# Keys loaded one head at a time, and turned by a product with the unit matrix instead of a two-head transpose

## Chip, cores, metric

One NeuronCore of a Trainium2 chip runs the whole program. The metric is the device time of one execution in microseconds, as a median of several runs. TensorE is called PE here (its weight loads PEld), VectorE DVE, ScalarE ACT, GpSimd POOL and SyncE SP; SP issues nearly all transfers.

## What is computed

Attention with four batches, twelve heads, 448 positions and a head size of 64. The heads are mixed before and after the softmax, and the result runs through a two-layer network with SiLU.

```python
scores = scale * np.matmul(q, k.transpose(0, 1, 3, 2))     # q, k, v: (4, 12, 448, 64) float32
scores = np.einsum('bhij,hg->bgij', scores, w_pre)          # mix of heads
scores = scores - np.max(scores, axis=-1, keepdims=True)
attn = np.exp(scores)
attn = attn / (np.sum(attn, axis=-1, keepdims=True) + 1e-09)
attn = np.einsum('bhij,hg->bgij', attn, w_post)             # second mix
x = np.matmul(attn, v)                                      # then (batch*seq, heads*size)
h = x @ w_in
out = (h * (1.0 / (1.0 + np.exp(-h)))) @ w_out
```

## The kernel before

The program has three parts. An **opening** (to about 28 us) brings queries and keys of batch 0 into the core and makes the first scores. The **mixing part** (to about 420 us) walks through four batches of four query tiles each (120 or 100 query rows), in groups of ten query rows. The **network** (from there to the end) is a chain of 128x448 products, L624.

In the mixing part every pair of groups takes these steps: L399 mixes the scores of all heads (`mix_pair`, into `pp`), L405 takes the row maxima on DVE, L409 the exponentials on ACT, L437 mixes them again (`mix_pair_again`, into the one tile `pa`), and L446 copies `pa` out on ACT. Between them stand pieces of other work: L368 multiplies finished weights with values (`values`), L339 makes the scores of the next tile (`scores`, into `pqk`), L344 and L346 copy these to a buffer `st` (six of them), and a transfer, L351, spreads `st` over the partitions of a tile `g`, from which L399 reads. A buffer `st` is free again once its transfer has landed.

What the change touches is the way keys come in. `load_k_pair` (L238 to L249) issues one transfer for each head of a pair. Position 4p+j of a head goes to partition p (112 partitions, j from 0 to 3), so a head is 1 KB in a row in memory for each partition. In the core the two heads of a pair lie interleaved: for each j first 64 numbers of one head, then 64 of the other. The tile is `kn`, or a part of one of the four value tiles `v` while that is not in use, so the trace names some of these transfers and products by `v`. `prep_k` (L264 to L278) then makes four transposes a pair with PE: for each j a block of 112 partitions by 128 columns (both heads) becomes 128 partitions by 112 columns of a bank `pt`. L274 and L277 split that into a rounded part `kh` and a rest `kl`.

There are 24 pairs of heads. The six of batch 0 are loaded and turned in the opening, between the first scores. The six of each later batch are loaded (lists `early`) and turned (lists `work`) while the batch before is being mixed, at places that `put` fixes by group number; the order of the instructions on each engine is written out by the loop over the groups. SP works through its transfers in program order, and each of them waits on the semaphore of the eighth transfer before it, so that about eight are on the way at a time.

Of the kernel before, what the change touches and what calls it, by code (L numbers as in the profile page):

```python
# [8 lines left out]
F32 = mybir.dt.float32  # L9
# [13 lines left out]
def raw(ap):  # L23

    return ap.bitcast(F32)
# [78 lines left out]
def talking_heads_then_silu_mlp(  # L104
# [11 lines left out]
    nc = tc.nc  # L116
    ctx.enter_context(tc.manual_schedule())
    B, H, S, D = q.shape
# [8 lines left out]
    JT = 112  # L127
    NJ = S // JT
# [20 lines left out]
    ident = const.tile([128, 128], F32, name="ident")  # L149
# [18 lines left out]
    def pool(name, bufs, stack=ctx, **kw):  # L168
        return stack.enter_context(tc.tile_pool(name=name, bufs=bufs, **kw))
# [13 lines left out]
    nat = pool("nat", 2, early_p)  # L183
# [12 lines left out]
    def bank(p, name):  # L196
        if p is ps_a:
            turns.append(name)
            return pa[:, len(turns) % 2]
        return p.tile([128, 512], F32, name=name, tag="bank")  # L200

    v_tiles = [v2_p.tile([KV, 4, NJ, D], F32, name="v4", tag="v4") for _ in range(4)]
# [35 lines left out]
    def load_k_pair(b, h, queues=(nc.sync, nc.sync)):  # L238
        if h >= 4 if b == 0 else h // 4 != 1:
            x = (b * H + 8) // 4 % 4 if b else h // 4 - 1  # L240
            if x in zeroed:
                zeroed.remove(x)
            t = v_tiles[x][:JT, h % 4:h % 4 + 2].rearrange("p i j d -> p (i j d)")
            t = t.rearrange("p (j i d) -> p j i d", i=2, j=NJ)
        else:
            t = nat.tile([JT, NJ, 2, D], F32, name="kn", tag="kn")
        kns[b, h] = t
        for i in range(2):
            queues[i].dma_start(out=t[:, :, i, :], in_=k[b, h + i].rearrange("(p j) d -> p j d", p=JT))  # L249

    def load_v_quad(b, h):
        x = (b * H + h + 8) // 4 % 4
# [11 lines left out]
    def prep_k(b, h):  # L264

        pt = bank(banks[0], "pt")
        kn = kns.pop((b, h))
        for j in range(NJ):
            nc.tensor.transpose(pt[:, j * JT:(j + 1) * JT], kn[:, j].rearrange("p h d -> p (h d)"), ident[:JT, :JT])  # L269

        kh, kl = ks[b, h] = [k2_p.tile([128, S], F32R, name=x, tag=x) for x in ("kh", "kl")]

        def take_high():
            nc.scalar.copy(out=kh, in_=pt[:, :S])  # L274

        def take_low():
            nc.vector.tensor_sub(out=kl, in0=pt[:, :S], in1=raw(kh))  # L277
        return [(take_high, take_low)]  # L278
# [196 lines left out]
    for n in range(1, len(seq)):  # L475
        p0, p1 = first[n - 1], first[n]
        spread = (0, 0, 0, 0, 2, 2) if n == 1 else (-6, -5, -4, -2, -1, 0) if p1 - p0 == 12 else (-6, -5, -4, -3, -2, -1)
        for h in range(0 if n > 1 else 2 * NE, H, 2):
            i = p0 + spread[h // 2]
# [7 lines left out]
    for n, (b, ti) in enumerate(seq):  # L487
        if n:
            p0 = first[n - 1]
            if n > 2:  # L490
                put(first[n - 2], lambda n=n: load_q(n)[0](), lead=7, w=2.1)
            for hg, i in ((0, p0 - 9), (1, p0 - 8)):
                if n > 1:
                    put(i, prep_q, n, hg)
            if ti == 0:
                c0 = first[n - 2]
                for h, i, lead in zip(range(0, H, 2), (0, 1, 3, 5, 7, 9), (10, 10, 11, 12, 5, 6)):
                    put(c0 + i, load_k_pair, b, h, lead=lead, w=1.2)
                    put(c0 + i, prep_k, b, h)
        if ti == 0:  # L500
            for h in range(0, H, 4):
                put(first[n] + ((5, 6, 8) if n else (15, 16, 18))[h // 4], load_v_quad, b, h, lead=2, w=1.8)
# [23 lines left out]
    for h in range(0, 6, 2):  # L526
        load_k_pair(0, h, (nc.sync, nc.scalar))
    loads[1]()
    for h in range(6, H, 2):
        load_k_pair(0, h)  # L530
    steps = [(prep_q, 0, 0), (prep_k, 0, 0), (prep_k, 0, 2)]
    for h in range(0, H, 2):
        if h + 4 < H:
            steps.append((prep_k, 0, h + 4))
        steps += [(scores, 0, h)]
        if h == 0:
            steps.append((prep_q, 0, 1))
# [313 lines left out]
    for s, (kind, m, u, a) in enumerate(steps):  # L851
# [14 lines left out]
        p = None  # L866
        if s >= len(phs):
            p = bank(ps_h, "ph")
# [58 lines left out]
```

## Time and profile before

| | |
|---|---|
| median of 3 runs | 872.0 us (870.98 to 878.78) |
| the profiled execution | 876.44 us, span 874.7 us |
| PE busy | 828.4 us, 95% of the span |
| PEld, DVE, ACT, POOL busy | 656.0, 625.4, 526.5, 406.4 us |
| transfers | 132.89 MB in 162343 packets; 50409 packets under 512 B |

The span is the time between the first and the last instruction of the profiled execution. Busy shares are means over three parts with different limits, so they have to be read by stretches; the granted clock of PE stands beside them. A busy PE is one with a product in its pipeline, and how many products it gets through is read from their starts.

### The profile page before, as it was taken

Reading aid. Unit: us, or ns where it says so; the run is one execution under the profiler, and the core shown is the slowest. Engines: PE = TensorE matmul, PEld = TensorE weight load, DVE = VectorE, ACT = ScalarE, POOL = GpSimd, SP = SyncE. Lnnn points to the kernel's source line nnn. Section 1 sums busy time; section 2 is a strip of 40 time slices with the busy share of each in tenths; the row PEclk is TensorE's granted clock in tenths of the full one; section 3 lists DMA queues with packets and bytes.
Section 4 is the critical chain, followed back from the end, with each engine's and each line's share of the span. In section 5 each row is a group of like instructions: output and inputs, shape, how many; then the busy total and the mean of one; then the engine's idle time right before and its main releaser. Section 6 shows DMA issues by size and latency. Waiting matters only on the chain.

```text
span 874.7 us, 27490 instructions
## 1 busy us (share of the span) xinstructions
PE 828.4 (95%) x11058; PEld 656.0 (75%) x11058; DVE 625.4 (71%) x1218; ACT 526.5 (60%) x1178; POOL 406.4 (46%) x681
## 2 busy tenths in 40 slices
PE   7797999899998999899899999999999999999997
PEld 5355666567666666666599999988899889999986
DVE  5453777468775777675878899999988689984332
ACT  4575778578786878677756653324694245343242
POOL 6231445355454645463877577557742233133020
PEclk7999899899999999999999999999999999999999
DMA  7569677887788787874635453355331142112234
GB/s 143 167 182 193 185 212 218 219 216 196 209 242 229 220 219 211 228 214 151 188 104 184 144 167 118 118 151 155 107 94 49 35 114 71 38 49 73 73 85 106
DMA packets 162343, 132.89 MB, mean 152 GB/s; under 512 B 50409, under 2 KB 155861, under 8 KB 162215
## 3 DMA queue, kind: packets, MB, share of 16 engines
q1 hardware_dynamic: 158809, 129.39, 53.0%
q8 instruction: 87, 1.43, 0.7%
q0 software_dynamic: 544, 1.03, 0.5%
q10 hardware_dynamic: 2862, 0.71, 0.4%
q14 instruction: 41, 0.34, 0.1%
HBM read 64.01 MB, written 27.53 MB: 105 GB/s over the span
## 4 chain that ended last, share of the span: by engine, by line
PE 75%; DVE 9%; DMA 7%; ACT 4%; issue 2%; SPq 2%; POOL 1%; ACTq 0%; POOLq 0%; DVEq 0%
PE ph L624 41%; PE pa L437 8%; PE pp L399 8%; PE po L368 7%; PE pqk L339 7%; DMA g<-st 4%; ACT e L409 2%; DVE nm L405 1%; DVE g L824 1%; PE pt L269 1%; PE ptt L844 1%; ACT at L446 1%; DVE op L630 1%; DMA v<-in_v 1%; DVE cg L92 1%
## 5 line engine op out<-in xcount | busy, mean ns | idle before, releaser
L624 PE MATMUL ph<-op,wh 128*128 128x448 f32 x924 | 221.5, 368 | 2.4 <-DVE g L834 1.8
L610 POOL TENSOR_TENSOR wl<-wl,wh 128x512 fp32r<-128x512 f32 x84 | 122.0, 1467 | 152.8 <-ACT wh L609 152.3
L624 PEld LDWEIGHTS ph<-op,wh 128*128 128x128 f32 x924 | 171.6, 188 | 18.1 <-DVE g L834 2.1
L405 DVE TENSOR_REDUCE nm<-pp 128x1 f32<-128x448 f32 x184 | 106.1, 618 | 76.1 <-PE pp L399 75.7
L425 POOL TENSOR_SCALAR wr<-wpost,r 128x60 f32<-128x60 f32 x184 | 70.7, 397 | 177.5 <-DVE r L422 139.0
L409 ACT ACTIVATE e<-pp,nm 128x448 f32<-128x448 f32 x184 | 115.4, 631 | 51.1 <-DVE nm L405 48.8
L437 PEld LDWEIGHTS pa<-wr,e 64*64 64x64 f32 (+1 forms) x5888 | 96.7, 131 | 44.9 <-issue 26.5
L437 PE MATMUL pa<-wr,e 64*64 64x60 f32 (+1 forms) x5888 | 108.6, 219 | 14.4 <-ACT at L446 8.6
L624 PE MATMUL ph<-op,wl 128*128 128x448 f32 x462 | 118.9, 366 | 0.0
L399 PE MATMUL pp<-g,wpre 64*64 64x448 f32 x736 | 104.9, 591 | 9.6 <-ACT e L409 5.7
L66 POOL TENSOR_TENSOR cg<-cw,cg 128x256 f32<-128x256 f32 x96 | 75.8, 790 | 76.6 <-DVE cw L63 73.5
L624 PEld LDWEIGHTS ph<-op,wl 128*128 128x128 f32 x462 | 86.7, 188 | 7.5 <-POOL wl L610 0.5
L446 ACT COPY at<-pa 120x960 f32<-120x960 f32 x92 | 89.9, 978 | 3.2 <-PE pa L437 3.2
L368 PE MATMUL po<-at,v 120*64 120x120 f32 (+1 forms) x1536 | 88.1, 268 | 1.8 <-DMA v<-in_v 1.5
L368 PEld LDWEIGHTS po<-at,v 120*64 120x64 f32 x1536 | 77.4, 139 | 14.6 <-issue 5.1
L609 ACT CAST wh<-wl 128x512 fp32r<-128x512 f32 x84 | 51.1, 617 | 54.3 <-DMA wl<-wo_dram 27.2
L344 DVE COPY st<-pqk 120x448 f32<-120x448 f32 (+1 forms) x89 | 55.0, 618 | 36.5 <-PE pqk L339 17.5
L90 ACT ACTIVATE cg<-cg,ebias 128x256 int32<-128x256 int32 x96 | 49.6, 516 | 44.2 <-DVE cg L86 43.0
L92 DVE SCALAR_TENSOR_TENSOR cg<-cw,cg 128x256 int32<-128x256 int32 x96 | 56.2, 586 | 16.4 <-ACT cg L90 16.0
L624 PE MATMUL ph<-x,wh 128*128 128x448 f32 x252 | 64.7, 365 | 0.0
L339 PEld LDWEIGHTS pqk<-kh,qh 64*120 64x120 f32 (+1 forms) x186 | 19.0, 179 | 50.0 <-issue 17.7
L339 PE MATMUL pqk<-kh,qh 64*120 64x448 f32 (+1 forms) x186 | 47.6, 467 | 6.8 <-ACT st L346 5.4
(122 smaller groups left out, 1379.0 us busy)
## 6 DMA issues: line engine op xcount, KB each, us to landing
g<-st SPq DMA_DIRECT2D x132, 210.0 KB
cw<-in_moe_w_in SPq DMA_DIRECT2D x48, 256.0 KB
cw<-in_moe_w_out SPq DMA_DIRECT2D x48, 256.0 KB
wi_dram<-cg SPq DMA_DIRECT2D x24, 448.0 KB
wo_dram<-cg SPq DMA_DIRECT2D x24, 448.0 KB
wl<-wi_dram SPq DMA_DIRECT2D x42, 256.0 KB
wl<-wo_dram SPq DMA_DIRECT2D x42, 256.0 KB
g<-st SPq DMA_DIRECT2D x48, 175.0 KB
```

The lines of the kernel that those rows point to most:

```text
L66: nc.gpsimd.tensor_mul(out=e, in0=m, in1=e)
L92: nc.vector.scalar_tensor_tensor(out=e, in0=hi, scalar=-2 ** 31, in1=e, op0=ALU.bitwise_and, op1=ALU.bitwise_or)
L339: nc.tensor.matmul(ps[i][:m, :S], lhsT=q_[rows, hh, :m], rhs=k_[rows], start=(step == 0), stop=(step == 2))
L368: nc.tensor.matmul(po[i * D:(i + 1) * D, c * m:(c + 1) * m], lhsT=vs[b, h][:, i, j, :], rhs=ats[n][:, j, h + i, :m], start=(j == 0), stop= ...
L399: nc.tensor.matmul((self, other)[r].p[HP * c:HP * (c + 1), :S], lhsT=wpre[rows], rhs=gs[self.n][rows, o // R + c * np + p, :], start=True, ...
L405: nc.vector.tensor_reduce(out=self.nm, in_=self.p[:GP, :S], axis=AX.X, op=ALU.max, negate=True)
L409: nc.scalar.activation(out=self.e, in_=self.p[:GP, :S], func=AF.Exp, bias=self.nm, scale=1.0, accum_out=sums)
L425: nc.gpsimd.tensor_scalar(out=g.wr, in0=wpost.rearrange("p g i -> p (g i)"), scalar1=r[:, i:i + 1], scalar2=1.0, op0=ALU.mult, op1=ALU.mult)
L437: nc.tensor.matmul(half[64 * c:64 * c + m, s, j * GH:(j + 1) * GH], lhsT=g.e[rows, j * JT + c * JH:j * JT + c * JH + m], rhs=g.wr[rows], s ...
L446: nc.scalar.copy(out=ats[self.n].rearrange("p j g t -> p (j g) t")[:, :, o:o + 2 * R].rearrange("p x (c i) -> p x c i", i=RH), in_=pa[:KV] ...
L610: nc.gpsimd.tensor_sub(out=wl, in0=raw(wl), in1=raw(wh))
L624: nc.tensor.matmul(p[:, :T], lhsT=w, rhs=x, start=(n == 0), stop=(n == len(todo) - 1))
```

## The change

Each transfer now puts the four rows of a head that belong to a partition next to each other, so the two heads of a pair lie behind one another and a partition gets 1 KB of a head in one piece. The block of both heads for one j is then no longer one piece of 128 columns. Instead of one transpose for each j there are two ordinary float32 products, one for each head: the stationary operand is the head's block (112 partitions, 64 columns), the moving one the unit matrix of 112 columns, and the result goes to the head's half of the 128 partitions of `pt`.

```diff
-            t = v_tiles[x][:JT, h % 4:h % 4 + 2].rearrange("p i j d -> p (i j d)")
-            t = t.rearrange("p (j i d) -> p j i d", i=2, j=NJ)
+            t = v_tiles[x][:JT, h % 4:h % 4 + 2]
         else:
-            t = nat.tile([JT, NJ, 2, D], F32, name="kn", tag="kn")
+            t = nat.tile([JT, 2, NJ, D], F32, name="kn", tag="kn")
         kns[b, h] = t
         for i in range(2):
-            queues[i].dma_start(out=t[:, :, i, :], in_=k[b, h + i].rearrange("(p j) d -> p j d", p=JT))
+            queues[i].dma_start(out=t[:, i], in_=k[b, h + i].rearrange("(p j) d -> p j d", p=JT))
...
         for j in range(NJ):
-            nc.tensor.transpose(pt[:, j * JT:(j + 1) * JT], kn[:, j].rearrange("p h d -> p (h d)"), ident[:JT, :JT])
+            for i in range(2):
+                nc.tensor.matmul(pt[i * D:(i + 1) * D, j * JT:(j + 1) * JT], lhsT=kn[:, i, j], rhs=ident[:JT, :JT], start=True, stop=True)
```

On PE the opening reads so (a row is a run of equal instructions, with the size of the result; `v_131` is a value tile that holds keys):

```order
-L269 MATMUL pt<-ident,kn 128x112 x8
-L269 MATMUL pa<-ident,v_131 128x112 x4
+L269 MATMUL pt<-ident,kn 64x112 x16
+L269 MATMUL pa<-ident,v_131 64x112 x8
 L339 MATMUL pqk<-kh,qh 120x448 x2
 L339 MATMUL pqk<-kh,ql 120x448 x2
 L339 MATMUL pqk<-kl,qh 120x448 x2
```

Nothing changes place there; every set of four transposes has become eight products at the same point. On SP the first transfers were these (the size is partitions by pieces):

```order
L297 DMA qn<-in_q 120x6x64
L249 DMA kn<-in_k 112x4x64 x2
L249 DMA v_131<-in_k 112x4x64
L297 DMA qn<-in_q 120x6x64
L249 DMA v_131<-in_k 112x4x64 x2
L249 DMA v_132<-in_k 112x4x64 x4
```

In the changed kernel the same six rows read:

```order
L297 DMA qn<-in_q 120x6x64
L248 DMA kn<-in_k 112x256 x2
L248 DMA v_131<-in_k 112x256
L297 DMA qn<-in_q 120x6x64
L248 DMA v_131<-in_k 112x256 x2
L248 DMA v_132<-in_k 112x256 x4
```

The number and the order of the transfers are the same; each one has 112 pieces of 256 numbers where it had 448 of 64. DVE, ACT and POOL keep their instructions and their order.

## Rows read from the trace of the kernel before

**Rows 1.** The page: busy time of PE; shares of the last-ending chain by line.
```profile
PE 828.4 (95%) x11058; PEld 656.0 (75%) x11058; DVE 625.4 (71%) x1218; ACT 526.5 (60%) x1178; POOL 406.4 (46%) x681
...
PE ph L624 41%; PE pa L437 8%; PE pp L399 8%; PE po L368 7%; PE pqk L339 7%; DMA g<-st 4%; ACT e L409 2%; DVE nm L405 1%; DVE g L824 1%; PE pt L269 1%; PE ptt L844 1%; ACT at L446 1%; DVE op L630 1%; DMA v<-in_v 1%; DVE cg L92 1%
```

**Rows 2.** Busy times by stretch; last three columns PEclk, DMA share, GB/s.
```profile
4.00:8.00 4.00, 2.11 (x15) 1.52 (x15) 1.67 (x4) 1.99 (x5) 3.58 (x8) 0.98 1.31 186
8.00:12.00 4.00, 3.98 (x19) 2.83 (x19) 1.63 (x4) 1.72 (x5) 0.33 (x1) 0.50 1.01 148
12.00:16.00 4.00, 4.00 (x18) 2.50 (x19) 2.66 (x6) 1.85 (x4) 1.12 (x2) 0.50 0.52 145
...
75.00:88.00 13.00, 8.46 (x211) 6.16 (x207) 3.57 (x10) 5.77 (x16) 1.69 (x6) 0.94 0.98 213
88.00:100.00 12.00, 12.00 (x210) 7.43 (x210) 8.00 (x19) 8.39 (x22) 4.32 (x9) 0.79 0.66 186
...
300.00:320.00 20.00, 19.54 (x426) 13.92 (x427) 15.44 (x37) 16.61 (x40) 11.20 (x26) 1.00 0.87 230
```

**Rows 3.** Timeline of PE from 299 us: start, length, engine, line, tiles, shape, count.
```profile
299.84 0.60 PE L269 MATMUL pt<-ident,v 112*128 112x112 f32 x4
300.37 0.98 PE L399 MATMUL pp<-g,wpre 64*64 64x448 f32 x8
301.28 1.86 PE L368 MATMUL po<-at,v 120*64 120x120 f32 x32
303.07 1.16 PE L437 MATMUL pa<-wr,e 64*64 64x60 f32 x64
...
304.52 0.55 PE L269 MATMUL pt<-ident,kn 112*128 112x112 f32 x4
305.00 0.98 PE L399 MATMUL pp<-g,wpre 64*64 64x448 f32 x8
...
306.91 1.16 PE L437 MATMUL pa<-wr,e 64*64 64x60 f32 x64 [0.46 <-ACT at L446]
```

**Rows 4.** Timeline of PE from 255 us.
```profile
255.36 1.59 PE L368 MATMUL po<-at,v 120*64 120x100 f32 x32
```

**Rows 5.** The chain of work that ended last, opening: start, length, what.
```profile
2.73 5.16 DMA v<-in_k
...
8.03 0.98 PE pa L269 x4
...
18.04 1.33 PE pqk L339 x11
...
23.56 4.88 DMA g<-first
```

**Rows 6.** PE busy from 8 to 12 us with L269 alone, then PEclk.
```profile
8.00:12.00 4.00, 1.93 (x8) 0.50 1.01 148
```

**Rows 7.** Transfers from 0 to 8 us: ACT's queue, packets, MB, share.
```profile
q10 hardware_dynamic: 1392, 0.34, 22.9%
```

**Rows 8.** Transfers from 410 to 414 us: SP's queue.
```profile
q1 hardware_dynamic: 245, 0.24, 18.5%
```

**Rows 9.** Issues of the first scores' transfers by SP: shortest/median/longest ns, first and last start.
```profile
L351 SPq DMA_DIRECT2D g<-first x18: 748/748/1442, 11.0 to 28.8; - x18
```

**Rows 10.** Issues of key transfers by SP, the same columns.
```profile
L249 SPq DMA_DIRECT2D v<-in_k x31: 562/630/2118, 2.7 to 306.7; - x31
```

**Rows 11.** Timeline of SP to 110 us: issues, with their length.
```profile
65.16 5.12 SPq L249 DMA_DIRECT2D v<-in_k  x4
...
75.95 3.09 SPq L249 DMA_DIRECT2D kn<-in_k  x2
...
80.94 5.19 SPq L351 DMA_DIRECT2D g<-st  x6
```

**Rows 12.** Timeline at 87 us: who waited for what before it started.
```profile
87.31 0.53 ACT L346 COPY st<-pqk 100x448 f32<-100x448 f32 x1 [1.12 <-DMA g<-st]
...
87.89 0.69 PE L339 MATMUL pqk<-kh,qh 64*100 64x448 f32 x1 [4.54 <-ACT st L346]
```

## The prediction

> **What bounds the kernel now.** I read the page first: PE is busy for 95% of the span and holds the first places of the chain, and the transposes of the keys, L269, are 1% of that chain, some 9 us [rows 1]. So the change works on a small sum, and what it can cost or give back is a few microseconds on either side of it. Then I read the windows by stage, because the transposes lie in four places only: six sets of four in the opening and six in each of three stretches of the mixing part. In those stretches PE is the bound: from 300 to 320 us it is busy for 19.54 of 20 us [rows 2], and its timeline shows one piece of work behind the other [rows 3]. There a microsecond more on PE is a microsecond more in the end, and a transfer that lands sooner gives nothing.
>
> Two other places are not bound by PE. In the opening, PE waits for the third pair of heads: the chain holds 5.16 us of a key transfer and then PE from 8.03 us to the last scores, which SP then spreads, the last of them landing 4.88 us after 23.56 us [rows 5]. From 75 to 88 us the transfers are at a share of 0.98 and PE is busy for 8.46 of 13 us [rows 2]; the scores at 87.89 us waited 4.54 us, for a buffer that its transfer had not yet emptied [rows 12]. The reader is to see that key transfers stand in SP's queue just ahead of those that empty the buffers: four in 5.12 us, then two in 3.09 us, and only at 80.94 us the first of the six [rows 11].
>
> **What the change costs on PE.** A set of four transposes takes from its start to that of the next work 0.53 us after L437 and 0.48 us after the query transposes (299.84 to 300.37, 304.52 to 305.00) [rows 3]; I take 0.51. The new set is eight float32 products. The trace has their like in L368: blocks of 120 partitions by 64 columns, in turn on the one and the other half of the columns, with 120 or 100 columns moving. Such a float32 product has two rows in the trace, so 32 rows are 16 products. With 120 columns they take 1.79 us to the next start (301.28 to 303.07; the row's 1.86 us has a tail of 0.07 that overlaps) [rows 3], with 100 columns 1.59 - 0.07 = 1.52 us [rows 4], that is 0.0135 us a column. At 112 columns 32 rows come to 1.68 us, and a new set of 16 rows to half of that, 0.84 us, if all of it scales with their number. The line through the two points leaves 0.17 us at no columns; if that is a fixed cost of the change from one kind of work to another, a set is 0.76 + 0.17 = 0.93 us. I take 0.88, the middle. The extra is 0.88 - 0.51 = 0.37 us a set; the bounds are 0.84 - 0.53 = 0.31 and 0.93 - 0.48 = 0.45.
>
> There are 18 such sets in the mixing part. Three of them, one per batch, stand shortly before a place where PE waits for ACT for some 0.46 us (306.91, behind the set at 304.52) [rows 3]; that wait covers their extra, so long as ACT, which has two splits and a copy of `pa` to do there, stays the last to come. Fifteen sets at 0.37 us are 5.6 us; one of them lies between 88 and 100 us, where the granted clock is 0.79 in the mean [rows 2], so I say 5.7 us. Bounds: 15 x 0.31 = 4.7 and 18 x 0.45 = 8.1.
>
> DVE and ACT read `pt` as before and get it 0.37 us later; what they feed (`kh`, `kl`) is used groups later, so that costs nothing as long as ACT has its slack. The only new waits are on PE, one for each head instead of one for both; the head that lands last decides as before.
>
> **What the transfers give back.** On ACT's queue, which carries almost only keys in the first 8 us, 1392 packets fill 22.9% of 16 engines for 8 us, so one of 256 B takes 21 ns [rows 7]. From 410 to 414 us 245 packets of 1 KB fill 18.5% of 4 us, 48 ns each [rows 8]. So 1 KB of keys goes from 84 ns to 48 ns of one engine: a head of 448 rows from 448 x 21 / 16 = 0.59 us of all engines to 112 x 48 / 16 = 0.34 us.
>
> In the batches at 174 and 285 us nothing waits for these transfers, so there it is 0 us.
>
> From 60 to 88 us the queue is full. Eight heads save 8 x 0.25 = 2.0 us of transfer time, and SP stands 5.12 + 3.09 us in six of their issues [rows 11], where six at the median of 0.63 us would be 3.8 us [rows 10], so some 4.4 us of it is stall. The six transfers that empty the buffers then start 2 to 4 us sooner, and the wait of 4.54 us [rows 12] shrinks by as much. I take 2.5 us, the lower end plus a little of the clock: PE idled before its clock fell, and it is at 0.79 from 88 to 100 us [rows 2], which is 12 x 0.21 = 2.5 us of work lost. With a shorter idle stretch some of that need not happen. Bounds: nothing (if other transfers fill the room at once) and 4.0 + 2.5 = 6.5 us. What is late next is the value loads in the same queue.
>
> In the opening three pairs, 6 x 112 KB, must land before 8.03 us; they save 6 x 0.25 = 1.5 us, and I take 1.4. From there the price depends on the clock. From 8 to 16 us PE is busy for 7.98 of 8 us, and its clock is 0.50, the lower level of 1.2 GHz [rows 2]; in the first half of that 1.93 us are L269 [rows 6]. At that level the four sets behind the wait take about 1 us each now (0.98 for the first) [rows 5] and would take 1.7 (twice 0.84), so 0.7 us more each: 2.8 us more, less 1.4, is 1.4 us; the last pairs' scatters, though, are paced by SP rather than by PE, so about half of it, 0.7 us, reaches the end. At the upper level the work between 8.03 and 18.04 us, 10.0 us now [rows 5] and 12.8 with the extra, would take 6.4. Then SP is the next in line: the first scores come some 2 us sooner (1.4 by the keys, the rest by the clock), the first scatter is issued at 9.0 instead of 11.0 us, and eleven more at 0.75 us [rows 9] with a little between them put the twelfth at 18 to 19 us instead of 23.56 [rows 5], a gain of about 5.
>
> Here a rule of the Trainium skill bears on the choice. TensorE: Matmul & The Clock Gate, Part 4, says that work in transpose mode does not count as PE being busy in the way products do, so that the full clock does not engage for it. The rows at 8 to 16 us agree: a PE that is busy for 3.98 of 4 us stays at 0.50 while half of that is transposes [rows 2, 6]. By the rule the products would raise the clock, and the opening would gain about 5 us; without it, it would lose about 0.7.
>
> From the rows alone: the clock fell behind 4 to 8 us, where PE was busy 2.11 of 4 us [rows 2], and with keys 1.4 us sooner and sets twice as long PE would have nearly no gap there. So I take a gain, but not all of it: 3.5 us. Bounds: a loss of 0.7 and a gain of 5.
>
> **The sum.** 5.7 - 2.5 - 3.5 = -0.3 us against the profiled execution's 876.44 us, so 876.1 us. That execution lies 4.4 us above the median of the three runs; applied to the median of 872.0 the forecast is 871.7, rounded to 872. A run of this kernel differs from the next by up to 7.8 us, so about 1% is what a measurement can tell from no change.
>
> **The rivals.**
>
> First, that the two halves of the columns do not run beside each other. Then eight products take twice 0.88 us, 1.25 us a set more than now, since 16 rows follow one another: 18 x 1.25 = 22.5 us in the mixing part, where no wait covers that much, and some 4 us in the opening, less 2.5 us from 60 to 88 us: about 896 us. It makes the kernel slower by over 1% from a set of 1.3 us on: (8.7 + 6.0 given back) / 18 is 0.8 us more than 0.51. Against it stands L368, which has the same shape and does overlap; for it, that L368 adds up over j in one place while here every product starts anew in another. The Trainium skill has a rule on this side: TensorE: Matmul & The Clock Gate, Terms, calls transpose mode four times faster for float32. Four times the 0.48 us of a set would be 1.9 us, and the mixing part about 18 x 1.4 = 25 us longer. No row here sets a transpose beside a product of the same block.
>
> Second, that the products keep the clock up in the opening and that the room in the queue from 60 to 88 us is worth its full price. This is what the rule of Part 4 would do here, together with the upper bound of the queue: 4.7 - 6.5 - 5 = -6.8, so 865 us.
>
> Third, that the transfers are hidden anyway: other packets fill the room from 60 to 88 us and the clock in the opening falls as before. Then 5.7 to 8.1 plus 0.7 is left: 878 to 881 us.
>
> **How the numbers follow.** The forecast has 0.52, the third rival 0.20, the second 0.18, the first 0.10. The range reaches to the second and the third, with their bounds and some 2 us for the medians themselves: 863 to 881 us; the first rival and the far ends are left out. Faster by over 1% (below 863.3) would need the second rival with luck on top: 0.10. Slower by over 1% (above 880.7) is the first rival and the worst of the third: 0.14. Within 1%: 0.76.
>
> **What the profile after would show.** Right, if a set of L269 takes 0.84 to 0.96 us to the next start in the stretch around 300 us; if the key issues on SP take less than half as long between 65 and 79 us and the wait before the scores at about 87 us is 2 us or so; if the first pairs are turned without a wait and the clock from 8 to 16 us is above 0.50. Wrong on PE, if a set takes 1.7 us; wrong on the transfers, if the first mix of the opening still starts at 28 us and the wait at 87 us is still above 4 us. The sum would be wrong if the sets' extra hid behind ACT in more than three places, or if the mixing part changed its waits at the tile boundaries, which no row here prices.

## The result and the profile after

The changed kernel takes 882.0 us (median of 22 runs, 872.6 to 886.5), the kernel before 877.5 us in 22 runs beside it (871.0 to 887.8). The ratio is 1.0054 with a 95% interval of 1.0031 to 1.0077: 4.7 us more, 2.7 to 6.8. Ratios here, unlike the medians, leave out the runs that lie over 1.5% above the fastest of the same kernel (five of 22 before, two of 22 after; the means of all runs differ by 2.9 us). The forecast was 872 us with a range to 881 and 0.3 us of gain.

Two things lie in the miss. The kernel before stood at 872.0 us by the three runs that the forecast was applied to, and at 877.5 by 22: 5.5 us of the 10 are the sampling of its median. The rest is the change, 4.7 us by the ratio. The change itself is within 1%, as forecast, but its sign is clear of the interval, and it is the third rival's.

The page of the changed kernel (its profiled execution took 882.34 us), the lines that answer to [rows 1]:

```profile
span 880.6 us, 28064 instructions
PE 833.7 (95%) x11346; PEld 663.7 (75%) x11346; DVE 625.7 (71%) x1218; ACT 527.9 (60%) x1178; POOL 407.1 (46%) x681
...
PE ph L624 39%; PE pa L437 9%; PE po L368 8%; PE pp L399 7%; PE pqk L339 7%; DMA g<-st 4%; PE pt L269 2%; ACT e L409 1%; DVE op L630 1%; DVE g L824 1%; DVE nm L405 1%; DMA qn<-in_q 1%; DVE cg L92 1%; PE ptt L844 1%; ACT at L446 1%
```

PE has 288 rows of products more, 24 sets by 12, and L269 went from 1% to 2% of the chain. The windows by stage, to be laid beside [rows 2]:

```profile
4.00:8.00 4.00, 3.90 (x49) 3.25 (x50) 1.35 (x3) 1.39 (x4) 3.58 (x8) 1.00 1.16 222
8.00:12.00 4.00, 4.00 (x55) 2.88 (x53) 3.11 (x6) 2.96 (x7) 1.18 (x2) 1.00 0.46 120
12.00:16.00 4.00, 4.00 (x50) 2.99 (x45) 3.04 (x10) 2.62 (x6) 0.27 (x1) 1.00 0.65 183
75.00:88.00 13.00, 11.48 (x279) 7.90 (x269) 5.74 (x16) 6.66 (x16) 1.89 (x5) 1.00 0.82 224
88.00:100.00 12.00, 11.79 (x260) 8.33 (x256) 8.99 (x21) 10.21 (x26) 6.07 (x15) 1.00 0.78 206
```

Both places that were not bound by PE look better, just as the forecast wanted: from 8 to 16 us the clock is 1.00 instead of 0.50, and from 75 to 88 us PE is busy for 11.48 of 13 us instead of 8.46. Still the kernel is slower. The timeline of PE around 304 us, where [rows 3] had 0.48 us for a set after the query transposes:

```profile
304.06 0.99 PE L269 MATMUL pt<-ident,kn 112*64 112x112 f32 x16
304.98 0.98 PE L399 MATMUL pp<-g,wpre 64*64 64x448 f32 x8
305.89 0.53 PE L310 MATMUL pt<-ident,qn 120*128 120x120 f32 x3
306.63 1.32 PE L437 MATMUL pa<-wr,e 64*64 64x60 f32 x64 [0.21 <-ACT at L446]
```

A set of eight products takes 0.92 us to the next start. The wait for ACT behind it fell from 0.46 us [rows 3] to 0.21 us, so at this place the extra has been covered in part.

The timeline of SP, beside [rows 11]:

```profile
62.32 3.64 SPq L248 DMA_DIRECT2D v<-in_k  x4
...
69.27 1.35 SPq L248 DMA_DIRECT2D kn<-in_k  x2
...
71.20 2.31 SPq L248 DMA_DIRECT2D kn<-in_k  x2
...
75.11 5.13 SPq L351 DMA_DIRECT2D g<-st  x6
```

The issues of key transfers by SP (shortest, median, longest ns), beside [rows 10]:

```profile
L248 SPq DMA_DIRECT2D v<-in_k x31: 312/377/1353, 2.2 to 303.7; - x31
```

Four key transfers pass the queue in 3.64 us instead of 5.12, the six that empty the score buffers start at 75.11 us instead of 80.94, and an issue costs SP 0.38 us instead of 0.63. Of the 5.8 us by which the buffers are emptied sooner, 2.8 us were there at the first of these key transfers already (62.32 against 65.16 us); 3.0 us are the stretch itself. PE's waits for a score buffer (timeline of PE from 80 to 92 us) are 1.5 us together, where [rows 12] had 4.54:

```profile
82.16 0.44 PE L339 MATMUL pqk<-kh,qh 64*100 64x448 f32 x1 [1.33 <-ACT st L346]
85.39 0.44 PE L339 MATMUL pqk<-kh,qh 64*100 64x448 f32 x1 [0.19 <-ACT st L346]
```

The chain of work that ended last, opening (beside [rows 5]):

```profile
1.78 4.93 DMA kn<-in_k
...
7.74 0.77 PE pa L269 x16
...
12.27 3.77 issue
16.04 3.92 DMA qn<-in_q
...
20.00 0.53 PE pt L310 x3
20.53 0.81 PE pqk L339 x6
```

The first mix, in PE's timeline:

```profile
22.84 1.76 PE L399 MATMUL pp<-g,wpre 64*64 64x448 f32 x16 [0.87 <-DMA g<-first]
```

The third pair is turned at 7.74 us, right behind the second and without a wait, and PE is at full clock; from 12 us on the chain runs through the second query tile, which POOL loads, and no longer through PE at half clock.

### The profile page after: what moved, and what is told of

Its sections match the earlier page's. It is cut to its first block, busy times and chain, and to the rows that moved or that the text cites. A ratio compares the mean times of both kernels' runs of the same rounds, so it can differ in the third digit from the quotient of the medians.

```text
span 880.6 us, 28064 instructions
## 1 busy us (share of the span) xinstructions
PE 833.7 (95%) x11346; PEld 663.7 (75%) x11346; DVE 625.7 (71%) x1218; ACT 527.9 (60%) x1178; POOL 407.1 (46%) x681
## 4 chain that ended last, share of the span: by engine, by line
PE 73%; DVE 10%; DMA 8%; ACT 4%; issue 3%; POOL 1%; SPq 1%; ACTq 0%; DVEq 0%; POOLq 0%
PE ph L624 39%; PE pa L437 9%; PE po L368 8%; PE pp L399 7%; PE pqk L339 7%; DMA g<-st 4%; PE pt L269 2%; ACT e L409 1%; DVE op L630 1%; DVE g L824 1%; DVE nm L405 1%; DMA qn<-in_q 1%; DVE cg L92 1%; PE ptt L844 1%; ACT at L446 1%
## 5 line engine op out<-in xcount | busy, mean ns | idle before, releaser
L624 PE MATMUL ph<-op,wh 128*128 128x448 f32 x924 | 223.1, 370 | 3.3 <-DVE g L834 1.8
L624 PEld LDWEIGHTS ph<-op,wh 128*128 128x128 f32 x924 | 172.3, 189 | 20.0 <-DVE g L834 2.1
L437 PEld LDWEIGHTS pa<-wr,e 64*56 64x56 f32 (+1 forms) x5888 | 97.5, 131 | 46.7 <-issue 28.8
L437 PE MATMUL pa<-wr,e 64*56 64x60 f32 (+1 forms) x5888 | 110.2, 220 | 15.4 <-ACT at L446 6.8
L624 PE MATMUL ph<-op,wl 128*128 128x448 f32 x462 | 119.6, 367 | 0.0
L399 PE MATMUL pp<-g,wpre 64*64 64x448 f32 x736 | 101.4, 568 | 10.5 <-ACT e L409 6.9
L624 PEld LDWEIGHTS ph<-op,wl 128*128 128x128 f32 x462 | 87.2, 189 | 7.6 <-POOL wl L610 0.6
L609 ACT CAST wh<-wl 128x512 fp32r<-128x512 f32 x84 | 51.1, 618 | 53.6 <-DMA wl<-wi_dram 26.7
L624 PE MATMUL ph<-x,wh 128*128 128x448 f32 x252 | 64.9, 366 | 0.0
L339 PEld LDWEIGHTS pqk<-kh,qh 64*120 64x120 f32 (+1 forms) x186 | 18.1, 173 | 45.8 <-issue 15.3
L346 ACT COPY st<-pqk 120x448 f32<-120x448 f32 (+1 forms) x89 | 48.0, 539 | 6.2 <-DMA g<-st 6.0
```

The source lines that it names most:

```text
L339: nc.tensor.matmul(ps[i][:m, :S], lhsT=q_[rows, hh, :m], rhs=k_[rows], start=(step == 0), stop=(step == 2))
L399: nc.tensor.matmul((self, other)[r].p[HP * c:HP * (c + 1), :S], lhsT=wpre[rows], rhs=gs[self.n][rows, o // R + c * np + p, :], start=True, ...
L437: nc.tensor.matmul(half[64 * c:64 * c + m, s, j * GH:(j + 1) * GH], lhsT=g.e[rows, j * JT + c * JH:j * JT + c * JH + m], rhs=g.wr[rows], s ...
L624: nc.tensor.matmul(p[:, :T], lhsT=w, rhs=x, start=(n == 0), stop=(n == len(todo) - 1))
```

## The experiments

The theory after these traces: a set of products costs more than forecast and hardly anything of it is covered, and the gains of the opening and of the queue were read off one execution of the kernel before that was unusually slow at both places. The rivals: that the products are not to blame but the packets give nothing or harm (order of landing, other transfers moved), that the halves of the columns do run one after the other, and that the extra on PE is hidden and something in the network or a wait at a tile boundary costs the time.

### Each part alone

`pack_only`: packets of 1 KB, and four full-width transposes as before, over 128 numbers in a row.

```diff
+        t = v_tiles[x][:JT, h % 4:h % 4 + 2]        # as in the change
+        queues[i].dma_start(out=t[:, i], ...)
...
-            nc.tensor.transpose(pt[:, j * JT:(j + 1) * JT], kn[:, j].rearrange("p h d -> p (h d)"), ident[:JT, :JT])
+            nc.tensor.transpose(
+                pt[:, j * JT:(j + 1) * JT], kn.rearrange("p h j d -> p (h j d)")[:, 2 * j * D:2 * (j + 1) * D], ident[:JT, :JT])
```

> Part one alone: keys in packets of 1 KB, and four full-width transposes a pair as before; each transpose takes 128 numbers in a row of a partition, two rows of one head, so the keys come out mixed up and the scores are of other numbers. Theory A (the loss is the sets of products on PE, about 0.40 us each in the mixing part; the clock in the opening is held up by the products): the clock falls in the opening as before, the queue from 60 to 88 us gives its 2.5 us, so 1 to 4 us faster than before. Theory B (the new packets change which transfers collide later, and that is what costs): slower than before by 3 us or more. Theory C (sooner keys alone hold the clock up): 1.00 from 8 to 16 us and 5 us or more faster.

`products_only`: packets as before, eight products.

```diff
-            nc.tensor.transpose(pt[:, j * JT:(j + 1) * JT], kn[:, j].rearrange("p h d -> p (h d)"), ident[:JT, :JT])
+            for i in range(2):
+                nc.tensor.matmul(pt[i * D:(i + 1) * D, j * JT:(j + 1) * JT], lhsT=kn[:, j, i], rhs=ident[:JT, :JT], start=True, stop=True)
```

> Part two alone: old packets of 256 B, with products in place of transposes. Theory A: the clock from 8 to 16 us is above 0.50, the opening gains 2 to 4 us, the sets cost 7 us: 3 to 6 us slower than before. Theory B: no slower than before. Theory C: the clock falls in the opening as before, and it is 7 to 9 us slower.

`products_in_opening`: both parts, for batch 0 alone; batches 1 to 3 as before (the transfers have the same condition on `b`).

```diff
...
+            if b:
+                nc.tensor.transpose(pt[:, j * JT:(j + 1) * JT], kn[:, j].rearrange("p h d -> p (h d)"), ident[:JT, :JT])
+                continue
+            for i in range(2):
+                nc.tensor.matmul(pt[i * D:(i + 1) * D, j * JT:(j + 1) * JT], lhsT=kn[:, i, j], rhs=ident[:JT, :JT], start=True, stop=True)
```

> Both parts for batch 0 alone, old packets and transposes for the three later batches. Theory A: the opening of the changed kernel (first mix near 23 us), no sets of products in the mixing part and no gain in the queue: 3 to 6 us faster than before. Theory B: as before within 2 us, or faster by the opening too; it does not tell B from A, but whether the opening's gain lives to the end.

`halves_in_series`: the changed kernel with the loop over heads outside, so that four products on one half of the columns follow one another, and then four on the other.

```diff
-        for j in range(NJ):
-            for i in range(2):
+        for i in range(2):
+            for j in range(NJ):
```

> The changed kernel with the loop over the heads outside: four products on one half of the columns, then four on the other. If the halves run beside each other only when they take turns (theory A's price of a set, 0.9 us, is then that of an overlap), a set takes some 1.6 us and the kernel is 18 x 0.7 = 12 us slower than the changed kernel, 15 to 18 us slower than before. If the halves never overlapped and a set's time is something else: as the changed kernel, within 2 us.

Measured on one chip, beside 23 runs of the kernel before at 874.7 us:

| kernel | runs | median us, all runs | ratio, 95% interval |
|---|---|---|---|
| pack_only | 12 | 876.4 | 1.0043 (1.0010 to 1.0075) |
| products_only | 6 | 884.0 | 1.0135 (1.0103 to 1.0166) |
| products_in_opening | 12 | 877.3 | 1.0028 (0.9993 to 1.0063) |
| halves_in_series | 4 | 890.0 | 1.0228 (1.0169 to 1.0287) |

The products are what costs: alone they make the kernel 11.8 us slower (9.0 to 14.5), more than both parts together and more than the 3 to 6 us expected. The packets alone do not make it faster either: 3.8 us slower here (0.9 to 6.6), where 1 to 4 us faster was expected; a repeat follows below. The opening shows no gain that reaches the end: with both parts in batch 0 the kernel is 2.4 us slower, between a gain of 0.6 and a loss of 5.5, where the forecast had a gain of 3.5. That is one set of runs, and the repeat of `pack_only` on another chip came out 0.6% lower, so a gain of 1 or 2 us is not excluded.

The halves overlap, if they alternate. PE's timeline of `halves_in_series`:

```profile
302.16 1.42 PE L269 MATMUL pt<-ident,v 112*64 112x112 f32 x16
303.51 0.45 PE L339 MATMUL pqk<-kh,qh 64*100 64x448 f32 x2
...
305.54 1.42 PE L269 MATMUL pt<-ident,v 112*64 112x112 f32 x16
306.89 0.98 PE L399 MATMUL pp<-g,wpre 64*64 64x448 f32 x8
```

In series the same eight products take 1.35 us a set instead of 0.92; 24 times 0.43 us is 10.3 us, and by the two ratios it is 15 us slower than the changed kernel, give or take 6. So the first rival is wrong for the order that the change has, and its 1.7 us was too much even for the other.

### The kernels before and after, profiled again

Three more profiled executions of unchanged kernels, to see how much of the first traces belongs to the execution and not to the kernel.

> The kernel before, unchanged, profiled once more. Theory A' (the half-speed stretch of the opening in the first profile belongs to that execution, whose mean clock of 0.977 is the lowest but two of some twenty, and not to the kernel): the clock from 8 to 16 us may well be 1.00 here, and then the first mix starts 3 to 5 us before 28.6 us with the old transposes. Theory A (the transposes keep the clock down): 0.50 from 8 to 16 us again.

> The same kernel, a third profile, for how far the opening, the wait near 87 us and the waits at the tile boundaries differ from one execution of one kernel to the next. Theory A': at least one of the two looks has the opening at full clock, and the waits differ by some us. Theory A: both at 0.50.

> The changed kernel once more. Both theories: sets of products of 0.91 to 0.94 us in the mixing part. Theory A: the opening at 1.00 again. Theory A': it may be at either level.

They took 866.56, 873.23 and 881.68 us. Windows of the second profiled execution of the kernel before (`before_second_look`), whose code is the same as in [rows 2]:

```profile
8.00:12.00 4.00, 3.23 (x24) 2.11 (x25) 2.87 (x7) 2.44 (x6) 0.73 (x2) 1.00 0.78 147
12.00:16.00 4.00, 3.87 (x32) 2.70 (x32) 3.64 (x11) 3.29 (x7) 0.72 (x1) 1.00 0.64 167
75.00:88.00 13.00, 10.96 (x267) 7.44 (x268) 6.44 (x17) 7.38 (x17) 2.29 (x6) 1.00 0.78 212
88.00:100.00 12.00, 11.53 (x236) 7.85 (x235) 9.18 (x22) 10.34 (x25) 5.69 (x13) 1.00 0.89 241
```

Three of these windows in the third (`before_third_look`):

```profile
8.00:12.00 4.00, 3.86 (x18) 2.71 (x19) 2.08 (x4) 2.04 (x5) 0.21 (x1) 1.00 1.07 150
...
75.00:88.00 13.00, 9.40 (x181) 5.82 (x172) 5.64 (x15) 6.28 (x16) 2.46 (x5) 0.89 0.85 223
88.00:100.00 12.00, 11.52 (x292) 8.57 (x292) 8.83 (x20) 9.75 (x23) 6.05 (x15) 0.98 0.84 234
```

In the same execution, the four transposes of the third pair (shortest, median, longest ns, first and last start):

```profile
L269 PE MATMUL pa<-ident,v x4: 391/391/418, 8.1 to 8.7; 112*128 112x112 f32 x4
```

The stretch of 10 us at half clock in the opening, on which the largest term of the forecast rested, was that execution's own. In the second PE is at full speed there with the old transposes (259 ns a row). In the third it is slow for the first part, 391 ns a row, until 12.7 us, and then fast. The idle time of PE from 75 to 88 us is 4.5 us in the first profiled execution, 2.0 and 3.6 us in the other two; 1.5 us in the changed kernel, 0.9 in its second execution.

In the second execution the chain through the opening is that of the changed kernel's first:

```profile
8.38 0.57 PE pa L269 x4
...
12.72 3.99 issue
16.70 4.00 DMA qn<-in_q
...
21.61 1.41 PE pqk L339 x6
...
24.16 1.77 PE pp L399 x8
```

So without the slow stretch both run there through the load of the second query tile, and what the keys give is small: the third pair is turned 0.6 us sooner (8.38 to 7.74 us), the second query tile starts to come in 0.7 us sooner (16.70 to 16.04) and the first mix starts 1.3 us sooner (24.16 to 22.84). The last 0.6 us of this are not the keys': in the second execution PE is at half clock from 20 to 24 us, and takes 1.41 us for six scores that take 0.81 in the changed kernel. In the third execution, and in the second of the changed kernel, the chain does not hold that load; it runs through POOL's work and then SP's scatters of the first scores.

### What a set costs at the end

`sets_thrice`: the changed kernel with each of the 18 later sets made three times; `transposes_thrice`: the same with the kernel before and its transposes. What the 36 extra sets add is the price of one in the end, covered or not.

```diff
-        for j in range(NJ):
+        for j in (x for _ in range(3 if b else 1) for x in range(NJ)):
```

> The changed kernel with each of the 18 sets of the mixing part made three times over, into the same place. If a set is wholly on the path (theory A): 36 more sets of about 0.9 us, less the three per 18 that hide behind ACT by 0.46 us at most, so 29 to 33 us slower than the changed kernel, 33 to 38 us slower than before. If the waits at the tile boundaries take up part of what PE loses: clearly less, 15 to 25 us over the changed kernel.

> The kernel before with each of the 18 sets of transposes of the mixing part made three times over, the counterpart of sets_thrice. Theory A (on the path a set of transposes costs what its starts show, 0.5 us, a set of products 0.9): 36 more sets give 15 to 18 us over before, so 0.42 to 0.5 us each, and the difference to the products' price times 18 sets is the 6 to 8 us that the change costs in the mixing part. Rival (what stands around a set takes up part of either price, and the loss comes from elsewhere): the two prices differ by less than 0.2 us.

> The changed kernel with its 18 later sets made three times, again, on the same chip as transposes_thrice, for the price of a set of products: 26 to 33 us over the changed kernel, 30 to 38 over before.

The first took 908.5 us beside 875.8 (4 runs; 1.0361, 1.0265 to 1.0458). On another chip, beside 877.5 us in 23 runs, the products took 907.6 us (6 runs; 1.0341, 1.0306 to 1.0377) and the transposes 886.2 us (6 runs; 1.0101, 1.0065 to 1.0137). The 36 extra sets of transposes cost 8.9 us, 0.25 us each (0.16 to 0.33), half of what was expected; those of products 29.9 us less the 4.7 us of the change itself, 0.70 us each, give or take 0.10. A threefold set of products in PE's timeline of `sets_thrice_again`:

```profile
328.79 2.52 PE L269 MATMUL pt<-ident,kn 112*64 112x112 f32 x48
331.24 0.98 PE L399 MATMUL pp<-g,wpre 64*64 64x448 f32 x8
```

And one of transposes, in that of `transposes_thrice`:

```profile
303.87 1.31 PE L269 MATMUL pt<-ident,kn 112*128 112x112 f32 x12
305.12 0.98 PE L399 MATMUL pp<-g,wpre 64*64 64x448 f32 x8
```

Three sets of products take 2.45 us, the second and third 0.77 us each; of that 0.70 reach the end. So nearly nothing of a set of products is hidden. Three sets of transposes take 1.25 us, and of some 0.39 us for each of the added ones 0.25 reach the end. The difference at the end, 0.45 us a set, times 18 is 8.2 us for the mixing part, give or take 2.4; by the timelines it is 0.92 - 0.51 = 0.41 us and 7.4 us. The forecast had 5.7, bounds to 8.1.

Not all of the loss stands in the mixing part. In the network, whose instructions are the same, PE takes 1.0 us longer at one place, near 543 us, in all eight executions that have one set of products for each later pair (3.2 to 3.3 us from the start of row 486 of L624 to that of row 497, against 2.23 in the ten others). It waits there for weights, which ACT casts at L609 once their transfer `wl` has landed. ACT's timeline, before and after:

```profile
537.65 0.62 ACT L609 CAST wh<-wl 128x512 fp32r<-128x512 f32 x1 [5.76 <-DMA wl<-wi_dram]
```

```profile
541.83 0.62 ACT L609 CAST wh<-wl 128x512 fp32r<-128x512 f32 x1 [7.37 <-DMA wl<-wi_dram]
```

PE's timeline after, and the queue of program code among the transfers from 536.5 to 541.8 us (packets, MB, share):

```profile
543.42 0.92 PE L624 MATMUL ph<-op,wl 128*128 128x448 f32 x3
544.89 1.27 PE L624 MATMUL ph<-op,wh 128*128 128x448 f32 x5 [0.55 <-DVE g L823]
```

```profile
q8 instruction: 1, 0.02, 1.0%
```

In those eight executions a packet of 16 KB of program code starts 2.4 to 2.5 us after the issue of that weight load, and the cast starts 5.2 us after the issue; in the ten others the cast starts 3.5 to 3.9 us after it, and no code packet starts between the two, but for one 0.1 us ahead of the cast in `transposes_thrice`. The 288 rows more on PE make the program longer (89 code packets instead of 87) and move the places at which code is fetched. No run moved a code packet alone, so the cause is read from the coincidence.

### What the packets give

`q_from_scalar`: the kernel before with the second query tile loaded from ACT's queue instead of POOL's, since the chain named it.

```diff
-            for load in load_q(1, nc.gpsimd, 2):
+            for load in load_q(1, nc.scalar, 2):
```

> The kernel before, with the queries of the second tile loaded from ACT's queue instead of POOL's, where the second half is issued 3.8 to 4.0 us after the first. In the second look at the kernel before and in the changed kernel the chain of the opening runs through that load once PE is at full clock. If it is what bounds the opening there: the first mix starts 1 to 2 us sooner and the kernel is 0 to 2 us faster than before. If SP's scatters bound it just behind: no change.

> Packets of 1 KB with full-width transposes, which mix up the keys' rows (the scores are of other numbers), a second time, since the first stood 1.7 us above before where 1 to 4 us below were expected. If the packets give nothing that lives to the end: within 2 us of before. If they cost (theory B): 2 us or more above it again. If the first was chance: 2 us or more below.

`q_from_scalar` took 878.2 us (12 runs; 0.9992, 0.9952 to 1.0031) beside 877.5: the end did not move. Its trace shows what stood right behind: the second half of the tile was turned at 19.78 us, and the first mix waited for the scatter of the first scores.

```profile
25.59 3.09 PE L399 MATMUL pp<-g,wpre 64*64 64x448 f32 x16 [3.84 <-DMA g<-first]
```

`pack_only` took 874.6 us this time (12 runs; 0.9982, 0.9940 to 1.0024). Its two ratios lie on both sides of one, and the first lay clear above it; that the packets without the products give a gain is not shown, and neither is a loss.

The last four went together on one chip, beside 22 runs of the kernel before at 877.3 us: the changed kernel, the products with the old packets, and the products with the new packets in batch 0 alone (`products_packets_first`) or in batches 1 to 3 alone (`products_packets_later`, with the conditions the other way round).

```diff
-            nc.tensor.matmul(..., lhsT=kn[:, i, j], ...)
+            nc.tensor.matmul(..., lhsT=kn[:, j, i] if b else kn[:, i, j], ...)
...
-            queues[i].dma_start(out=t[:, i], ...)
+            queues[i].dma_start(out=t[:, :, i, :] if b else t[:, i], ...)
```

> Products everywhere, packets of 1 KB for batch 0 alone. Theory A (what the packets give beside the products comes from the opening, where sooner keys close PE's gaps): as the changed kernel, 4 to 6 us over before. Theory D (it comes from the queue between 60 and 88 us): as products_only, 8 to 11 us over before.

> Products everywhere, packets of 1 KB for batches 1 to 3 alone. Theory A: as products_only, 8 to 11 us over before. Theory D: as the changed kernel, 4 to 6 us over before.

> Products with packets of 256 B on the same chip as the two, for the difference. Theories A and D: 8 to 11 us over before, 4 to 5 over after_again. If the first measurement was chance: as after_again within 2 us.

> The changed kernel on the same chip as the three: 4 to 6 us over before by all theories.

| kernel | runs | median us, all runs | ratio, 95% interval |
|---|---|---|---|
| products_only_again | 6 | 884.5 | 1.0101 (1.0029 to 1.0174) |
| products_packets_first | 6 | 881.3 | 1.0109 (1.0051 to 1.0166) |
| products_packets_later | 12 | 881.7 | 1.0068 (1.0029 to 1.0107) |
| after_again | 11 | 879.9 | 1.0067 (1.0025 to 1.0109) |

The medians of all runs fall by some 3 us with the packets in either place and by 4.6 with both; by the ratios the packets of the opening give nothing, those of the later batches 3 us, and both together 3 us. All these intervals overlap. That the packets give something beside the products, and how it is divided, stays open by these four. No version was faster than the kernel before by more than its interval.

The traces of all these kernels do show what the packets do at their two places. The first mix of the opening (first start of L399) is at 28.6, 24.1, 24.7 and 24.7 us in the four executions whose opening is that of the kernel before, at 24.3 to 24.8 us in three with products and old packets, and at 22.6 to 23.8 us in seven with products and new packets (`halves_in_series`, whose sets are longer, is not among them). In the median that is 24.7 against 22.9 us, 1.8 us. The products have no part in that: with the new packets and the old transposes (`pack_only`, twice) it is at 23.2 and 23.4 us. The first of these, in its chain:

```profile
23.22 1.83 PE pp L399 x8
```

PE's waits for a score buffer before the products L339 from 80 to 90 us are 1.1 to 4.5 us where the later batches have old packets (nine executions, mean 2.6) and 0 to 1.5 us where they have new ones (six, mean 0.8): 1.8 us. A seventh of these, the repeat of `pack_only`, waited 2.9 us; with it the mean is 1.1 and the difference 1.5 us. The two executions with sets made three times are left out.

## Why the prediction was wrong

**The clock in the opening, the step that failed.** "So I take a gain, but not all of it: 3.5 us" was the largest of the gains, and its price rested on [rows 2], where PE is at 0.50 from 8 to 16 us, and on the chain of [rows 5]. The place was right: the keys land sooner, the third pair is turned without a wait, the clock is 1.00 and the first mix starts at 22.84 instead of 28.63 us. But other executions of the same opening start it at 24.1 to 24.7 us, because the clock came up sooner or did not fall, and the change then gives 1.8 us at the first mix. At the end, batch 0 with both parts gave no gain (2.4 us slower, a gain of 0.6 at most by its interval): the forecast's 3.5 us lie outside it. Where the 1.8 us go between the first mix and the end was not found; later stretches at half clock fall at different places (from 44 us in the changed kernel's first trace, from 32 us in its second).

The forecast applied that gain to the median, though it was computed against one execution. The bounds were a loss of 0.7 and a gain of 5, and a value near the upper one was taken; in the four other executions with this opening or its first 16 us the slow stretch is 3 to 5 us long, or absent, and there are no 10 us to give back.

**The products.** The forecast of 0.88 us a set was 0.04 short (0.92 measured, inside its bounds of 0.84 to 0.93, and the fixed part that it halved is there nearly in full: 0.77 for a further set on the spot, and 0.15 more for the first). Of the 18 sets it let three hide behind ACT; by the sets made three times nearly all of a set reaches the end, although at 304 us a part of the wait did take some of it up. Together 7.4 to 8.2 us instead of 5.7, at the upper bound; the interval of the 8.2 reaches down to 5.8.

**The network.** The forecast put it at nothing, and did not name it. PE loses 1.0 us there, with the code packet that falls into the flight of a weight load. That is chance of position: with two more sets of products for each pair (`sets_thrice`, twice) no packet falls there, and the 1.0 us are not lost.

**The queue from 60 to 88 us.** The mechanism is as forecast: shorter issues, the buffers emptied earlier, a shorter wait of PE. One of its signs failed: the six key issues were to take less than half as long, and took 5.95 us (3.64 and 2.31) instead of 8.21 [rows 11]. The 2.5 us came out as 1.5 to 1.8 us in the mean of the executions, since the wait of 4.54 us [rows 12] was the longest of nine.

**The sum.** 7.4 for the sets and 1.0 for the network less 1.8 for the queue is 6.6 us if the opening gives nothing at the end, and 4.8 if its 1.8 arrive; measured were 4.7 (2.7 to 6.8). The forecast is 5.0 us off. The opening is 1.7 to 3.5 of that, the sets 1.7, the network 1.0 and the queue 0.7, so the opening's part is the largest, or level with that of the sets. One figure does not fit well: 8.2 us for the sets, the network's 1.0 and the 2.4 us of the opening together would leave 7 us to the later packets, which is more than the 1.8 us that their row shows; the first and the last have intervals of some 3 us.

**The range.** Its upper end, 881, was to hold the third rival with its bounds and some 2 us for the medians; the third rival alone reaches 880.8, so the 2 us are not in it. They were too few, too: the median of three runs lay 5.5 us under that of 22.

**The rivals.** The first is refuted by the timelines (0.92 us; 1.35 us when the order keeps the halves apart). The rule of the Trainium skill on its side, TensorE: Matmul & The Clock Gate, Terms, with four times the speed for float32 in transpose mode, is not seen in this size: a set costs 0.92 us against 0.51, 1.8 times, and further sets on the spot 0.77 against 0.39, twice; with the halves in series 1.35 us is 2.6 times.

The third came nearest, 878 to 881 us from 872, 6 to 9 us more. In part that is luck: 4.7 us more lies below it, and only the low median of three runs brings 882.0 close to its upper end. Its reason, that the transfers change nothing, is wrong for what the traces show at both places; whether it holds at the end stays open.

The second has the time wrong; whether the products bring the clock up, its mechanism, is settled in part. With the old packets PE ran slow from 8 us on, by the durations of its weight loads, in four of five executions with transposes (until 11, 11, 12.7 and 18 us) and in one of three with products. With the new packets it stayed fast in all ten, two with transposes and eight with products. So the new packets are enough, and whether the products alone would do it stays open. In `pack_only` PE is busy throughout from 8 to 12 us, at full clock (windows):

```profile
8.00:12.00 4.00, 4.00 (x33) 2.51 (x31) 3.58 (x8) 3.23 (x8) 1.45 (x2) 1.00 0.61 168
```

And three sets of transposes lie in those 4 us (PE's timeline):

```profile
8.70 0.62 PE L268 MATMUL pt<-ident,v 112*128 112x112 f32 x4
10.05 0.60 PE L268 MATMUL pt<-ident,v 112*128 112x112 f32 x4
11.39 0.60 PE L268 MATMUL pt<-ident,v 112*128 112x112 f32 x4
```

The rule of the Trainium skill in TensorE: Matmul & The Clock Gate, Part 4, that work in transpose mode does not count as a busy PE in the same way, would have the clock low there, as the prediction used it; these rows, and the second execution of the kernel before, speak against it as the cause. What differs with the packets is that PE waits less ahead of 8 us (busy 2.11 of 4 us in [rows 2], 3.52 and 3.18 in `pack_only` and its repeat). That this is the cause is not shown: the second execution of the kernel before was busy for 2.52 us there and stayed fast. A kernel with transposes and a gap that is filled by other work was not run.

## What to carry to other kernels

Price a gain from the clock against several executions of the kernel before, not against the one that happens to be profiled: a cold stretch of 10 us in one trace was absent or much shorter in the others, and more than half of the forecast's gains hung on it. Where PE is the bound, an edit that trades transposes for products on it was paid nearly in full here (0.70 of 0.77 us a set), and to multiply the piece (here three times) prices it at the end far better than a difference of 5 us can. A longer program may cost time where nothing was changed: compare the untouched parts of the two traces, too. Faster transfers gave the start and the queue a part of what the trace promised, and less than the products took: count both in the same currency, time of the engine that ends last.

## What the runs showed of the hardware

- Float32 products on the two column halves overlap more when they alternate, even if each starts anew in its own place: 0.92 us for eight in turn, 1.35 us for four and four.
- A packet of 1 KB of keys took 52 ns of a DMA engine in the first 8 us (384 packets, 15.7% of 16 engines), where four of 256 B had taken 84 [rows 7]. SP's issue got shorter too, 0.38 instead of 0.63 us, for the same bytes.

```profile
q10 hardware_dynamic: 384, 0.34, 15.7%
```

- The granted clock of a window can read 1.00 while PE still runs slow: in the third execution of the kernel before the transposes at 8.1 us took 391 ns a row, about as long as the 394 ns at the lower level (the first execution, at 8.0 us), in a window that is put down at 1.00. At the start of a program the durations of equal instructions tell the level more safely than that column.
- A packet of 16 KB of program code in the flight of a weight load of 256 KB goes with a cast that starts 5.2 instead of 3.5 to 3.9 us after the issue (eight executions against ten), and PE stood 1.0 us longer for it.
- The kernel before took from 867 to 888 us in about 95 runs on several chips, with mean granted clocks from 0.977 to 0.993 in its three profiled executions (874.7, 871.5 and 864.8 us of span). A change of a few microseconds is not seen in one run of each.
